# Recurrent-memory attention and a gated FFN on one core: own and early value tiles merged for 64-row products, and the normalisation of the segment outputs divided between VectorE and ScalarE

## The chip, the core and the metric

The kernel runs on one core of a Trainium2 chip. Its engines are TensorE (PE; its weight loads are a row of their own, PEld), VectorE (DVE), ScalarE (ACT), GpSimd (POOL) and the sequencer SyncE (SP), which issues most of the DMAs. The metric is the device time of one execution in microseconds; less is better. Three runs of the kernel before took 1026.67 to 1027.17 us, with a median of 1027.08.

## What is computed

A sequence of 2048 rows of 640 is normalised, cut into 64 segments of 32 rows, and run through attention with 32 heads of 128. Each segment has 8 memory rows ahead of its 32 own rows; the memory of a segment is the output of the segment before it at the memory rows, so the segments form a chain. Then a gated FFN of width 1728 follows.

```
mem = mem0
for s in range(n_seg):
    h = concat([mem, layernorm(x)[s]])           # 8 + 32 rows
    q, k, v = h @ Wq, h @ Wk, h @ Wv             # 32 heads of 128
    p = softmax(where(mask, q @ k.T * scale, -1e9))
    o = (p @ v) @ Wo
    mem, out[s] = o[:8], o[8:]
h  = x + out
h2 = h + ((relu(g) * u) @ W_down)                # g, u = layernorm(h) @ W_gate, @ W_up
```

(`gate * (gate > 0)` is written as `relu` here.)

## The kernel before

**Order of the work.** All operations are appended by `add` to one list, in program order; `_Graph.solve` works out the semaphore waits from the keys that an operation reads and writes, and each engine runs its own operations in that order. A wait on an engine therefore holds everything behind it on that engine, and so does a DMA that waits on SP. There is no planner: the order is the order of the calls.

**Own and early rows.** A segment's tile of projections has 32 columns: 8 memory rows and the first 24 of its 32 own rows. The last 8 rows of each of four segments, which do not depend on the memory, are projected ahead, for four segments together ("early", tiles `Ke`, `Qe`, `Ve`, `act_e`, two buffers each, one for a block of four). So keys and values of a segment come from two tiles: `Ko` and `Vp` (own, `a = 0`) and `Ke` and `Ve` (early, `a = 1`, of which a mask lets through the segment's own rows and those ahead of it in the block). The early projections, and for every fourth segment a pass `woe_pass` over outputs, are cut into three parts and put between the steps of the chain (`filler`).

**Layout.** Heads stand as `head(k, g)`: `g` is a group of 32 partitions (0 to 3), `k` counts 0 to 7 within it. `Vp` and `Ve` are 128 x 8 x 130: partition group `g` has the 32 rows of the values of that group's heads, column 128 is 1 (it gives the softmax's sum). `Px` holds the exponentials, 128 x 512: own ones in columns 0 to 255, early ones in 256 to 511.

**A segment (the loop over `s` from line 898 on), around the change:**

1. K is projected in two halves (`project`, matmuls on lines 374 and 357); ScalarE copies each half from PSUM to `tok[0]`, `tok[1]` (`to_tok`, line 395) and VectorE transposes it into `Ko` (`flip`, line 390).
2. `pv_x(s - 1, 0)`, line 638: the outputs of the 32 query rows of the segment before. For each of two halves `kh`, for own and early, for four columns `c` of the array and four row groups `g`, one product of 32 rows x 32 columns with 129 moving columns: 64 products, own and early summed in PSUM, into banks 0 to 3. Then `norm_x`, line 648 (reciprocal) and line 651 (two multiplications into `ox`, 128x512 each), on VectorE.
3. Q is projected in two halves, copied to `tok[2]`, `tok[3]` by ScalarE and transposed into `Qo` by VectorE; then `flip_ox(s - 1, (0,))`, line 535, transposes the first half of `ox` into `oT`.
4. V half 0 is projected and copied to `Vp[s % 2]`; `scores(s, 0)` (line 460); V half 1; `scores(s, 1)`. `scores` writes own products to columns 0 to 159 and early ones to columns 160 to 319 of a bank, each head group to its partition group.
5. `exp_mem`, `mask_mem` (lines 476, 482), `flip_ox(s - 1, (1,))`, `pv_mem` (line 513, the outputs of the memory rows), `norm_mem`, `flip_mem`, `exp_x`, `mask_x` (line 494), the fillers.
6. The output projection `wo_split`, `wo_pass` (lines 572, 555) and `to_act_split` (lines 595, 596), which writes the next segment's memory rows; `rows_split` and `store_attn` send the rows to DRAM (`attn_d`, four DMAs on SP).

Segment 0 is written out ahead of the loop, with its `pv_x` and `norm_x` there, while the weights are still arriving; the loop calls `pv_x(s - 1, 0)` from `s = 2` on. The last `pv_x` is called behind the loop, on banks 4 to 7. In segments 35, 39, 43 and 47 a transposing load, a store to `xn2_d`, and loads of `xt` and `at` for the FFN's first rows go through SP; in the segment after each, POOL adds `xt` and `at` and SP stores the sum to `h_d`.

```python
for kh in range(2):
    for a in range(2):
        for c in range(4):
            k = 4 * kh + c
            for g in range(4):
                pe.matmul(bank(b0 + g)[32*c:32*c+32, 129*kh:129*kh+129],
                          Px[32*g:32*g+32, 256*a + 32*k:256*a + 32*k + 32],
                          (t0, t1)[a][32*g:32*g+32, k, 0:129], start=(a == 0), stop=(a == 1), ...)
```

Of the kernel before, what the change touches and what calls it, by code (L numbers as in the profile page):

```python
# [163 lines left out]
def build_kernel(nc, A_x, A_mem0, A_Wq, A_Wk, A_Wv, A_Wo, A_seg_len, B_W_gate, B_W_up, B_W_down, out):  # L164
# [57 lines left out]
    mca = ar.alloc("mca", [128, 5, SEG], BF16)  # L222
    act_r = [ar.alloc(f"act_r{i}", [128, 4, DC, 32], BF16) for i in range(2)]
    act_e = [ar.alloc(f"act_e{i}", [128, DC, 32], BF16) for i in range(2)]
    tok = [ar.alloc(f"tok{i}", [128, 512], BF16) for i in range(4)]
# [5 lines left out]
    Vp = [ar.alloc(f"Vp{i}", [128, 8, VW], BF16) for i in range(2)]  # L231
# [8 lines left out]
    ox = ar.alloc("ox", [128, 4, 2, Dh], BF16)  # L240
    wtok = [ar.alloc(f"wtok{i}", [128, DC, 32], BF16) for i in range(2)]
# [36 lines left out]
    for i in (1, 0):  # L278
        add("pool", lambda p, i=i: p.memset(wtok[i][:], 0.0), w=[("wtok", i)])
# [4 lines left out]
    for i in range(2):  # L284
        add("dve", lambda v, i=i: v.memset(oT[i][:], 0.0), w=[("oT", i, n, kh) for n in "mx" for kh in range(2)])
        add("pool", lambda p, i=i: p.memset(act_r[i][:], 0.0),
            w=[("act", i, j, "m") for j in range(4)] + [("act", i, "x")] + [("act", i, "x", j) for j in range(4)])
        add("pool", lambda p, i=i: p.memset(ap(Vp[i], Dh, [[VW, 8], [1, VW - Dh]]), 1.0), w=[("Vp1", i)])
        add("pool", lambda p, i=i: p.memset(ap(Ve[i], Dh, [[VW, 8], [1, VW - Dh]]), 1.0), w=[("Ve1", i)])
        add("pool", lambda p, i=i: p.memset(act_e[i][:], 0.0), w=[("acte", i)])  # L290

    add("pool", lambda p: p.memset(mca[:], BIG), w=[("mca",)])
    for g in range(4):
        for n in range(5):
            sl = mca[32 * g:32 * g + 32, n, :]
            add("pool", lambda p, sl=sl, n=n: p.affine_select(sl, sl, [[1, SEG]], ALU.is_ge, 0.0,
                                                              base=M if n == 0 else M * (n - 1) - RID,
                                                              channel_multiplier=-1), r=[("mca",)], w=[("mca",)])
            if n > 1:
                add("pool", lambda p, sl=sl, n=n: p.affine_select(sl, sl, [[0, SEG]], ALU.is_ge, 0.0,  # L300
                                                                  base=-M * (n - 1), channel_multiplier=1),
                    r=[("mca",)], w=[("mca",)])
    add("pool", lambda p: p.memset(mbd[:], 0.0), w=[("mbd",)])
    for g in range(4):
        add("pool", lambda p, g=g: p.memset(mbd[32 * g:32 * g + 32, :, 8 * g:8 * g + 8], BIG), r=[("mbd",)], w=[("mbd",)])
        for n in range(1, 5):
            sl = mbd[32 * g:32 * g + 32, n, :]
            add("pool", lambda p, sl=sl, n=n: p.affine_select(sl, sl, [[0, 32]], ALU.is_ge, 0.0, base=-M * (n - 1),
                                                              channel_multiplier=1), r=[("mbd",)], w=[("mbd",)])
            add("pool", lambda p, sl=sl, n=n: p.affine_select(sl, sl, [[0, 32]], ALU.is_ge, 0.0, base=M * n - 1,  # L310
                                                              channel_multiplier=-1), r=[("mbd",)], w=[("mbd",)])
# [51 lines left out]
    def project(act, akeys, j, halves, banks, chunks=range(5)):  # L363

        def f(pe):
            for c in chunks:
                for n, i in enumerate(halves):
                    for g in range(4):
                        o = 2048 * i
                        w = (W[:, j, c, o + 512 * g:o + 512 * g + 512] if j == 2 else  # L370
                             W[:, j, c, o:o + 2048].rearrange("p (h e) -> p h e", e=128)[:, :, 32 * g:32 * g + 32])
                        a = (bank(banks[n])[32 * g:32 * g + 32, :], act[:, c, :], w)
                        if n == 0 or not HOLD:
                            ins = pe.matmul(*a, start=(c == 0), stop=(c == DC - 1), skip_group_check=True)  # L374
                        else:
                            ins = again(pe, *a, c == 0, c == DC - 1, g)
            return ins
        add("pe", f, r=list(akeys) + [("W", j, c) for c in chunks], w=[B(b) for b in banks] + [("Wdone", j)])

    def to_tok(b, t, eng):  # L380
        copy_op(eng, tok[t][:, :], bank(b), [B(b)], [("tok", t)])
# [7 lines left out]
    def flip(t, dst, i, keys):  # L389
        add("dve", lambda v: v.transpose(dst[:, 16 * i:16 * i + 16, 0:32], tok[t][:, :].rearrange("p (h f) -> p h f", f=32)),  # L390
            r=[("tok", t)], w=keys)
# [58 lines left out]
    def scores(s, hf):  # L450
# [3 lines left out]
        def f(pe):  # L454
            for k in range(4 * hf, 4 * hf + 4):
                for a in range(2):
                    for g in range(4):
                        h = head(k, g)
                        o = 160 * a + 40 * (k % 4)
                        i = pe.matmul(bank((P0, P1)[hf])[32 * g:32 * g + 32, o:o + 40],  # L460
# [13 lines left out]
    def exp_mem(s, hf):  # L474
        _, j = place(s)
        add("act", lambda a: a.activation(ap(Pm, 32 * hf, [[64, 2], [8, 4], [1, 8]]), s_view(hf, 0, M), ACTF.Exp,
                                          scale=SCALE), r=[B((P0, P1)[hf])], w=[("Pm", hf)])

    def mask_mem(s, hf):
        _, j = place(s)  # L480
        for i in (1, 0):
            add("dve", lambda v, i=i: v.tensor_tensor(ap(Pbd, 256 * i + 128 * hf, [[32, 4], [8, 4], [1, 8]]),
                                                      ap(Pm, 64 * i + 32 * hf, [[8, 4], [0, 4], [1, 8]]),
                                                      ap(mbd, 32 * (1 + j) * i, [[0, 4], [8, 4], [1, 8]]), ALU.min),
# [7 lines left out]
    def mask_x(s):  # L492
# [3 lines left out]
                                             ap(mca, 0, [[32 * (1 + j), 2], [0, 8], [1, 32]]), ALU.min),  # L496
            r=[("Px", 0), ("Px", 1), ("mca",)], w=[("Px", 0), ("Px", 1)])

    def v_of(s, a):
        par, p = s % 2, place(s)[0]  # L500
        if a == 0:
            return Vp[par], [("Vp", par, i) for i in range(2)] + [("Vp1", par)]
        return Ve[p], [("Ve", p, i) for i in range(2)] + [("Ve1", p)]

    def pv_mem(s, hf):
# [10 lines left out]
        (vp, e), par = place(s), s % 2  # L516
        add("pe", f, r=[("Pbd", a, hf) for a in range(2)] + [("Ve", vp, hf), ("Ve1", vp), ("Vp", par, hf), ("Vp1", par)],
# [14 lines left out]
    def flip_ox(s, halves=(0, 1)):  # L532
        p = (s + 1) % 2
        for kh in halves:
            add("dve", lambda v, kh=kh: v.transpose(ap(oT[p], 160 * kh + M, [[320, 4], [40, 4], [1, 32]]),  # L535
                                                       ap(ox, 128 * kh, [[256, 4], [1, 4], [4, 32]])),
                r=[("ox", kh)], w=[("oT", p, "x", kh)])
# [90 lines left out]

    def pv_x(s, b0):
        (t0, k0), (t1, k1) = v_of(s, 0), v_of(s, 1)  # L630

        def f(pe):
            for kh in range(2):
                for a in range(2):
                    for c in range(4):
                        k = 4 * kh + c
                        for g in range(4):
                            i = pe.matmul(bank(b0 + g)[32 * c:32 * c + 32, 129 * kh:129 * kh + 129],  # L638
                                          Px[32 * g:32 * g + 32, 256 * a + 32 * k:256 * a + 32 * k + 32],
                                          (t0, t1)[a][32 * g:32 * g + 32, k, 0:129], start=(a == 0), stop=(a == 1),  # L640
                                          skip_group_check=True, tile_position=(32 * g, 32 * c))
            return i
        add("pe", f, r=[("Px", 0), ("Px", 1)] + k0 + k1, w=[B(b0 + g) for g in range(4)])

    def norm_x(b0):
        src = ps[:, b0 * 512:b0 * 512 + 2048].rearrange("p (g r) -> p g r", r=512)[:, :, 0:258].rearrange(
            "p g (k d) -> p g k d", d=129)
        add("dve", lambda v: v.reciprocal(rx[:, :].rearrange("p (g k) -> p g k", k=2), src[:, :, :, 128]),
            r=[B(b0 + g) for g in range(4)], w=[("rx",)])
        for kh in range(2):  # L650
            add("dve", lambda v, kh=kh: v.tensor_tensor(ox[:, :, kh, :], src[:, :, kh, 0:128],  # L651
                                                      ap(rx, kh, [[2, 4], [0, 128]]), ALU.mult),
                r=[B(b0 + g) for g in range(4)] + [("rx",)], w=[("ox", kh)])
# [35 lines left out]
    for g in range(4):  # L689
        dma(wtok[1][32 * g:32 * g + M, :, :],  # L690
            mem0_ap.rearrange("t (c g j) -> g t c j", g=4, j=32)[g], r=[("wtok", 1)], w=[("wtok0", g)], eng="act")
# [18 lines left out]
    copy_op("dve", w0, wtok[1][:].rearrange("p c t -> p (c t)"), [("wtok", 1)] + [("wtok0", g) for g in range(4)],  # L710
# [156 lines left out]
    for n in range(2):  # L867
        for i in range(2):
            to_v(OB[2][n][i], Vp[0] if n else Ve[1], i, ("Vp", 0) if n else ("Ve", 1), ("act", "dve")[i])
# [3 lines left out]
    pv_x(0, P0)  # L873
# [4 lines left out]
    norm_x(P0)  # L878
    flip_ox(0)
# [18 lines left out]
    for s in range(1, NSEG):  # L898
# [16 lines left out]
        if s > 0:  # L915
            a, ks = pass_act(s)
            for i in range(2):
                project(a, ks, 1, (i,), ((P2, P3)[i],))
                to_tok((P2, P3)[i], i, "act")
                if last and i == 1:  # L920
                    load_piece(("tok", i), "act")
# [10 lines left out]
            if s > 1:  # L932
                pv_x(s - 1, 0)
                norm_x(0)
# [5 lines left out]
            if s > 1:  # L940
# [5 lines left out]
            to_v(P2, Vp[par], 0, ("Vp", par), "act")  # L946
            if last:
                load_piece(("Vp", par, 0), "act")
# [10 lines left out]
        if last:  # L959
            to_v(P3, Vp[par], 1, ("Vp", par), "act")  # L960
# [12 lines left out]
        if s > 0:  # L973
            if s > 1:
                flip_ox(s - 1, (1,))
            to_v(P3, Vp[par], 1, ("Vp", par), "act")
# [41 lines left out]
        if s >= 1:  # L1018
            rows_split(P3, P1, wtok[par], ("wtok", par))
            store_attn(wtok[par], ("wtok", par), M, 32 * (s - 1), RID)  # L1020
# [111 lines left out]
    norm_x(P0)  # L1132
    flip_ox(s)
# [109 lines left out]
```

## Time and profile before

| | |
|---|---|
| median of 3 runs | 1027.08 us (1026.67 to 1027.17) |
| the profiled execution | 1026.84 us, its span 1025.1 us |
| granted TensorE clock, mean | 0.998 |
| VectorE, ScalarE, GpSimd busy | 716.0, 501.5, 168.8 us |
| `pv_x`, line 638 | 4096 products, 4% of the chain that ended last |
| projections, line 374 | 47% of that chain |

The profile shows one execution. A group line gives the source line, engine, operation, tiles written and read, shapes and count; the timeline gives the same in order of time with start and length; the chain view follows back, from the last instruction, what each step waited for. A matmul line's form "128*32 128x512" means 128 rows and 32 columns of the array, 128 partitions and 512 columns of moving data. Starts of matmuls are recorded; their ends are modelled, and consecutive matmuls overlap.

### The profile page before, as it was taken

The page shows a single profiled execution, that of the slowest core. Times are in us where ns is not written, and L with a number is a line of the kernel's source. Part 1 is how long each engine was busy: PE and PEld are TensorE (multiplying, and loading weights), DVE is VectorE, ACT ScalarE, POOL GpSimd, SP SyncE. Part 2 cuts the span into 40 slices and gives each one's busy share as a digit, 9 for nine tenths or more (in the row PEclk, how much of TensorE's full clock was granted, in tenths as well). Part 3 has the DMA queues.
Part 4 walks back from the last instruction along what each step waited for, and adds up shares of the span by engine and source line. Part 5 has one row for each costly group of instructions (what it writes and reads, how often), then busy time and mean ns, then how long its engine had stood idle before and what let it go on. Part 6 is the DMA issues. An engine that isn't in the chain of part 4 may idle for free.

```text
span 1025.1 us, 57915 instructions
## 1 busy us (share of the span) xinstructions
PE 994.6 (97%) x27201; PEld 559.5 (55%) x26104; DVE 716.0 (70%) x1796; ACT 501.5 (49%) x1262; POOL 168.8 (16%) x402
## 2 busy tenths in 40 slices
PE   4789999999999999999999999999999999999998
PEld 1255656565656565656565566656565554444443
DVE  2558787878778787888888778787777765355332
ACT  1345555555555555565556555555555542121220
POOL 6020202120202020222222222121210010000000
PEclk9999999999999999999999999999999999999999
DMA  9920100010001001111212111000000048413100
GB/s 372 416 68 6 21 7 21 7 22 7 21 7 22 7 21 12 29 18 23 46 27 32 28 32 22 20 8 16 9 6 8 8 114 242 130 27 90 27 14 26
DMA packets 58531, 52.23 MB, mean 51 GB/s; under 512 B 37840, under 2 KB 55216, under 8 KB 56368
## 3 DMA queue, kind: packets, MB, share of 16 engines
q1 hardware_dynamic: 56160, 47.23, 16.7%
q8 instruction: 208, 3.41, 1.4%
q10 hardware_dynamic: 2128, 1.31, 0.5%
q14 instruction: 35, 0.29, 0.1%
HBM read 37.04 MB, written 6.55 MB: 43 GB/s over the span
## 4 chain that ended last, share of the span: by engine, by line
PE 93%; SPq 3%; DMA 2%; issue 0%; DVE 0%; ACT 0%; DVEq 0%; ACTq 0%
PE ps L374 47%; PE ps L817 11%; PE ps L555 7%; PE ps L572 7%; PE ps L357 6%; PE ps L638 4%; PE ps L615 4%; SPq L320 3%; PE ps L1049 3%; PE ps L460 3%; DMA Wo<-in_A_Wo_dram 2%; PE ps L513 2%; PE ps L830 0%; PE ps L1061 0%; DVE TBf L595 0%
## 5 line engine op out<-in xcount | busy, mean ns | idle before, releaser
L374 PE MATMUL ps<-W,act_r 128*32 128x512 bf16 x7580 | 448.3, 381 | 2.1 <-DVE act_r L596 1.4
L374 PEld LDWEIGHTS ps<-W,act_r 128*32 128x32 bf16 x7580 | 190.6, 96 | 201.5 <-DVE act_r L596 31.2
L395 ACT ACTIVATE tok<-ps 128x512 bf16<-128x512 f32 x324 | 189.0, 597 | 163.5 <-PE ps L374 134.4
L374 PE MATMUL ps<-W,act_e 128*32 128x512 bf16 x1224 | 121.2, 383 | 7.5 <-DMA W<-in_A_Wv_dram 4.0
L468 POOL COPY Qo<-Qe 128x256 bf16<-128x256 bf16 x64 | 31.8, 497 | 547.4 <-DVE oT L529 524.4
L390 DVE STREAM_TRANSPOSE Ko<-tok 128x512 bf16<-128x512 bf16 x128 | 89.6, 701 | 40.0 <-ACT tok L395 36.9
L395 ACT ACTIVATE Vp<-ps 128x512 bf16<-128x512 f32 x127 | 75.8, 597 | 69.2 <-PE ps L374 69.2
L390 DVE STREAM_TRANSPOSE Qo<-tok 128x512 bf16<-128x512 bf16 x126 | 88.9, 706 | 14.1 <-ACT tok L395 14.1
L535 DVE STREAM_TRANSPOSE oT<-ox 128x512 bf16<-128x512 bf16 x128 | 87.8, 687 | 0.0
L357 PE MATMUL ps<-W,act_e 128*32 128x512 bf16 x856 | 87.7, 385 | 0.0
L555 PE MATMUL ps<-Wo,oT 128*32 128x160 bf16 x4032 | 83.3, 233 | 1.0 <-issue 0.6
L651 DVE TENSOR_TENSOR ox<-ps,rx 128x512 bf16<-128x512 f32 x128 | 82.5, 687 | 2.2
L572 PE MATMUL ps<-Wo,oT 128*32 128x320 bf16 x2016 | 81.2, 299 | 0.0
L555 PEld LDWEIGHTS ps<-Wo,oT 128*32 128x32 bf16 x4032 | 75.7, 97 | 5.8 <-DMA Wo<-in_A_Wo_dram 1.3
L585 ACT ACTIVATE SA<-TA 64x40 f32<-64x40 f32 x126 | 29.5, 234 | 84.9 <-DVE TA L583 84.2
L845 ACT ACTIVATE g<-ps 128x512 bf16<-128x512 f32 x52 | 30.1, 593 | 82.8 <-PE ps L817 82.8
L817 PE MATMUL ps<-xn2T,Wu 128*128 128x512 bf16 x260 | 64.6, 379 | 0.0
L846 DVE TENSOR_TENSOR hT<-g,ps 128x512 bf16<-128x512 bf16 x52 | 35.8, 688 | 40.5 <-PE ps L817 40.1
L572 PEld LDWEIGHTS ps<-Wo,oT 128*32 128x32 bf16 x2016 | 56.4, 96 | 13.8 <-issue 1.1
L374 PEld LDWEIGHTS ps<-W,act_e 128*32 128x32 bf16 x1224 | 37.1, 97 | 47.8 <-issue 34.8
L817 PE MATMUL ps<-xn2T,Wg 128*128 128x512 bf16 x246 | 61.6, 379 | 1.5 <-issue 1.1
L529 DVE STREAM_TRANSPOSE oT<-om 128x128 bf16<-128x128 bf16 x126 | 39.2, 311 | 29.4 <-ACT om L524 28.1
(109 smaller groups left out, 1359.1 us busy)
## 6 DMA issues: line engine op xcount, KB each, us to landing
W<-in_A_Wk_dram SPq DMA_DIRECT2D x5, 1024.0 KB
W<-in_A_Wq_dram SPq DMA_DIRECT2D x5, 1024.0 KB
W<-in_A_Wv_dram SPq DMA_DIRECT2D x5, 1024.0 KB
Wo<-in_A_Wo_dram SPq DMA_DIRECT2D x8, 640.0 KB
attn_d<-wtok SPq DMA_DIRECT2D x248, 7.5 KB
xt<-in_A_x_dram SPq DMA_DIRECT2D x16, 160.0 KB
at<-attn_d SPq DMA_DIRECT2D x16, 160.0 KB
out_dram<-osb SPq DMA_DIRECT2D x15, 160.0 KB
```

Of the source, the lines that this page charges most:

```text
L357: return pe.add_instruction(mybir.InstMatmult(name=nc.get_next_instruction_name(), engine=mybir.EngineType.PE, ins=[pe.lower_ap(rhs), pe.l ...
L374: ins = pe.matmul(*a, start=(c == 0), stop=(c == DC - 1), skip_group_check=True)
L390: add("dve", lambda v: v.transpose(dst[:, 16 * i:16 * i + 16, 0:32], tok[t][:, :].rearrange("p (h f) -> p h f", f=32)), r=[("tok", t)], w= ...
L395: add("act", lambda a: a.activation(dst, src, ACTF.Copy), r=r, w=w)
L529: add("dve", lambda v: v.transpose(ap(oT[par], 160 * hf, [[40, 4], [320, 4], [1, 8]]), ap(om, 128 * hf, [[1, 4], [4, 32]])), r=[("om", hf) ...
L535: add("dve", lambda v, kh=kh: v.transpose(ap(oT[p], 160 * kh + M, [[320, 4], [40, 4], [1, 32]]), ap(ox, 128 * kh, [[256, 4], [1, 4], [4, 3 ...
L555: i = pe.matmul(bank(bk)[32 * gg:32 * gg + 32, 0:160], src[:, hb, 0:32], w[:, gg], start=(hb == CH[16 * halves[0]]), stop=(hb == CH[-1]), ...
L572: i = pe.matmul(bank(bk)[32 * q:32 * q + 32, 0:320], src[:, hb, 0:32], w, start=(n == 0), stop=(n == 7), skip_group_check=True)
L615: ins = pe.matmul(bank(bk)[32 * q:32 * q + 32, 0:320], src[:, hb, 0:32], w[:, 2 * (q % 2):2 * (q % 2) + 2], start=(i == 0), stop=(i == 15) ...
L638: i = pe.matmul(bank(b0 + g)[32 * c:32 * c + 32, 129 * kh:129 * kh + 129], Px[32 * g:32 * g + 32, 256 * a + 32 * k:256 * a + 32 * k + 32], ...
L651: add("dve", lambda v, kh=kh: v.tensor_tensor(ox[:, :, kh, :], src[:, :, kh, 0:128], ap(rx, kh, [[2, 4], [0, 128]]), ALU.mult), r=[B(b0 + ...
L817: ins = pe.matmul(bank(bk), w[:, c, lo:lo + 128], xn2T[par][:, c, :], start=(c == 0), stop=(c == DC - 1))
```

## The change

- `merge_v`: DMAs on SP copy own and early values into two merged tiles `VM[0]`, `VM[1]` of 128 x 8 x 130. `VM[r]` has, in partition group `g`, the own values where `g % 2 == r` and the early values elsewhere. To make neighbouring groups belong to the same heads, the early V projection swaps neighbouring groups (`swap`), and `scores` writes early products of group `g` to partition group `g ^ 1` and sorts its columns by `g % 2`. One `merge_v` is four DMAs of 32 partitions. The own ones are called in each segment once both halves of `Vp` are written, the early ones in every fourth segment behind `pv_x`.
- `pv_x` then takes 64 rows at a time, 32 products, with no sum in PSUM. The masks `mca`, `mbd` are laid out anew (more instructions on POOL at the start), and `exp_mem` and `mask_mem` address by the new order, with the same element counts.
- `norm_x` keeps the reciprocal and the first multiplication. The second is cut: `norm_x_late` multiplies half of it on VectorE and the other half in two ScalarE copies with a scale. It is called, with `flip_ox(s - 1, (0,))`, between the two halves of the Q projection; before, `flip_ox` came behind both.
- Segment 0's `pv_x` and `norm_x` move into the loop (`s = 1`).
- Space: `ox` shares a tile `tox` with `tok[0]` and `tok[1]`; `Vp` and `wtok` have one buffer instead of two.

```diff
     def project(act, akeys, j, halves, banks, chunks=range(5)):
+        swap = 1 if j == 2 and akeys[0][0] == "acte" else 0
...
-                        w = (W[:, j, c, o + 512 * g:o + 512 * g + 512] if j == 2 else
+                        w = (W[:, j, c, o + 512 * (g ^ swap):o + 512 * (g ^ swap) + 512] if j == 2 else
...
                 for a in range(2):
                     for g in range(4):
                         h = head(k, g)
-                        o = 160 * a + 40 * (k % 4)
-                        i = pe.matmul(bank((P0, P1)[hf])[32 * g:32 * g + 32, o:o + 40],
+                        o, q = 160 * (g % 2) + 40 * (k % 4), 32 * (g ^ a)
+                        i = pe.matmul(bank((P0, P1)[hf])[q:q + 32, o:o + 40],
...
+    def merge_v(s, a):
+        (t, ks), flat = v_of(s, a), "p k d -> p (k d)"
+        for r in range(2):
+            for g in range(4):
+                if g % 2 == r ^ a:
+                    dma(VM[r][32 * g:32 * g + 32].rearrange(flat), t[32 * g:32 * g + 32].rearrange(flat), r=ks,
+                        w=[("VM", r, g)])
...
             for kh in range(2):
-                for a in range(2):
+                for r in range(2):
                     for c in range(4):
                         k = 4 * kh + c
-                        for g in range(4):
-                            i = pe.matmul(bank(b0 + g)[32 * c:32 * c + 32, 129 * kh:129 * kh + 129],
-                                          Px[32 * g:32 * g + 32, 256 * a + 32 * k:256 * a + 32 * k + 32],
-                                          (t0, t1)[a][32 * g:32 * g + 32, k, 0:129], start=(a == 0), stop=(a == 1),
-                                          skip_group_check=True, tile_position=(32 * g, 32 * c))
+                        for u in range(2):
+                            i = pe.matmul(bank(b0 + 2 * u + r)[32 * c:32 * c + 32, 129 * kh:129 * kh + 129],
+                                          Px[64 * u:64 * u + 64, 256 * r + 32 * k:256 * r + 32 * k + 32],
+                                          VM[r][64 * u:64 * u + 64, k, 0:129], start=True, stop=True,
+                                          skip_group_check=True, tile_position=(64 * u, 32 * c))
...
+    def norm_x_late(b0):
+        src = ps[:, b0 * 512 + 1024:b0 * 512 + 2048].rearrange("p (g r) -> p g r", r=512)[:, :, 129:257]
+        add("dve", lambda v: v.tensor_tensor(tox[:, 2:4, 1, :], src, ap(rx, 5, [[2, 2], [0, 128]]), ALU.mult),
+            r=[B(b0 + 2), B(b0 + 3), ("rx",)], w=[("ox", 1, 1)])
+        for g in range(2):
+            add("act", lambda a, g=g: a.activation(tox[:, g, 1, :], bank(b0 + g)[:, 129:257], ACTF.Copy,
+                                                   scale=rx[:, 2 * g + 1:2 * g + 2]),
+                r=[B(b0 + g), ("rx",)], w=[("ox", 1, 0)])
...
-            if s > 1:
-                pv_x(s - 1, 0)
-                norm_x(0)
+            pv_x(s - 1, 0)
+            norm_x(0)
+            if s % 4 == 2:
+                merge_v(s, 1)
             if not last:
                 for i in range(2):
                     project(a, ks, 0, (i,), ((P0, P1)[i],))
                     to_tok((P0, P1)[i], 2 + i, "act")
                     flip(2 + i, Qo, i, [("Qo", i)])
-            if s > 1:
+                    if i == 0:
+                        norm_x_late(0)
+                        flip_ox(s - 1, (0,))
...
         if s > 0:
-            if s > 1:
-                flip_ox(s - 1, (1,))
-            to_v(P3, Vp[par], 1, ("Vp", par), "act")
+            flip_ox(s - 1, (1,))
+            to_v(P3, Vp, 1, ("Vp",), "act")
+            merge_v(s, 0)
```

## The prediction

> **What bounds the kernel now.** I read the page first: the engines' shares and the chain that ended last.
>
> ```profile
> span 1025.1 us, 57915 instructions
> PE 994.6 (97%) x27201; PEld 559.5 (55%) x26104; DVE 716.0 (70%) x1796; ACT 501.5 (49%) x1262; POOL 168.8 (16%) x402
> PE 93%; SPq 3%; DMA 2%; issue 0%; DVE 0%; ACT 0%; DVEq 0%; ACTq 0%
> ```
>
> TensorE (PE) carries 93% of the chain. What is not PE (SPq and DMA) lies ahead of 57 us, while the weights arrive. Next I asked for the chain in the middle of the recurrence, 300 to 360 us: every piece is PE, one behind another, and a segment takes 12.40 us.
>
> ```profile
> 305.86 2.21 PE ps L374 x40
> 308.07 0.66 PE ps L638 x64
> 308.73 3.35 PE ps L374 x60
> 312.08 0.25 PE ps L460 x31
> ```
>
> So in segments 2 to 63 a nanosecond off PE is a nanosecond off the span, until another engine is late. L638 is `pv_x`, 64 products of 32 rows each. Then the timeline of PE around that piece (columns: start, length, line, shapes, count), and the same in slices of 0.02 us; the two lines from slices are the ones with x6 and the x4 that starts at 307.68.
>
> ```profile
> 307.68 0.39 PE L374 MATMUL ps<-W,act_r 128*32 128x512 bf16 x4
> 308.00 0.24 PE L638 MATMUL ps<-Vp,Px 32*32 32x129 bf16 x6
> ...
> 308.00 0.28 PE L638 MATMUL ps<-Vp,Px 32*32 32x129 bf16 x16
> 308.07 0.28 PE L638 MATMUL ps<-Ve,Px 32*32 32x129 bf16 x16
> 308.25 0.35 PE L638 MATMUL ps<-Vp,Px 32*32 32x129 bf16 x16
> 308.38 0.35 PE L638 MATMUL ps<-Ve,Px 32*32 32x129 bf16 x16
> 308.66 3.42 PE L374 MATMUL ps<-W,act_r 128*32 128x512 bf16 x60
> ```
>
> The call has three parts. From the last start of L374 (307.69) to the first of L638 (308.00) 0.309 us pass: 512 columns (0.213, since four such products share a pitch of 0.215) and a pause of 0.096 that appears at no change between two 128*32 forms. Then 64 starts in 0.510. Then 0.153 to the next L374: 129 columns (0.054) and again 0.099. In all 0.972, the same to 1 or 2 ns in 61 of the 62 calls at L638 that stand between L374 (segment 54's took 1.113). Inside the 0.510, six products start within 0.02 us, one per 3.3 ns; the second round of sixteen starts 0.067 behind the first (129 columns and 0.013 more). After about 33 pairs of weight load and matmul nothing starts until 308.25, and from there one pair starts per 8.3 ns: whatever was queued is used up, and PE runs at the rate of its issue.
>
> **The PE term.** After the change the call has 32 products of 64 rows and 32 columns of the array: 8 places of the array, 4 rounds. The form 64*32 is not in the trace. The nearest rows are L638 itself and the only 64-row products, L1061.
>
> ```profile
> 924.19 0.30 PE L357 MATMUL ps<-Wd,hT 128*128 128x320 bf16 x1
> 924.43 0.45 PE L1061 MATMUL ps<-Wd,hT 64*128 64x320 bf16 x4
> 924.80 0.31 PE L1049 MATMUL ps<-Wd,hT 128*128 128x320 bf16 x1
> ```
>
> Here two products in the two row halves start together (924.43, x2 in a narrower window) and the next two 0.147 later: the halves do run beside each other, and a round is its 320 columns (0.133) plus 0.014. The changes of form cost 0.232 and 0.229, that is the columns and 0.096 to 0.099 as above. So I take for the new call 0.309 before, 3 rounds of 0.067 plus 7 starts of 0.0033 = 0.224 from first to last start, and 0.153 behind: 0.686 instead of 0.972, **0.286 less**. All 32 pairs fit into the 33 that were queued, so the slow issue does not show. Bounds: a round of 0.0565 if weight loads hide (L513, 129 columns, has about that pitch) gives 0.193 and a gain of 0.317; issue at 8.3 ns throughout gives 0.258 and 0.252. I take 0.067, the row of the same columns and tile width. Times 63 calls on the chain (segments 2 to 63 and the last one): 18.0 us, from 15.9 to 20.0.
>
> **What is moved.** The call for segment 0 stood at 45.21, under the Wo load (chain: DMA to 55.5 us), free. It moves into segment 1, which has no such call: 0.686 less the 0.205 that L374 takes anyway, **+0.48**, once (0 to 0.7).
>
> **scores.** Same 64 products a segment, but early ones swap the array's column groups, so a group comes again after 3 or 5 places instead of 4. At 838.00 a queued call shows 25 ns a round of four; one more start (3.3 ns) a round makes 8 rounds 0.226, and a call takes 0.241 from first to last start now, as its last pair is issued late. I take 0; a whole pair (8.3 ns) in each of 16 rounds would be 0.13 a segment. Fewer than none is excluded: nothing is taken out.
>
> **VectorE and ScalarE.** With `pv_x` at 308.00, today's rows:
>
> ```profile
> 308.75 0.71 DVE L390 STREAM_TRANSPOSE Ko<-tok 128x512 bf16<-128x512 bf16 x1 [0.37 <-ACT tok L395]
> 309.39 0.17 DVE L648 RECIPROCAL rx<-ps 128x8 f32<-128x8 f32 x1
> 309.59 1.29 DVE L651 TENSOR_TENSOR ox<-ps,rx 128x512 bf16<-128x512 f32 x2
> 310.79 0.70 DVE L390 STREAM_TRANSPOSE Qo<-tok 128x512 bf16<-128x512 bf16 x1
> 311.68 0.71 DVE L390 STREAM_TRANSPOSE Qo<-tok 128x512 bf16<-128x512 bf16 x1 [0.19 <-ACT tok L395]
> ```
>
> The reciprocal waits for the second K flip, not for PE, so it stays at 309.39. One product ends at 310.27. ScalarE has the first Q half out at 310.29 (0.29 sooner), so its flip runs 310.32 to 311.02. Then the late half-product (128x256; L602's 128x160 takes 0.325 and L1070's 128x320 0.485, so about 0.4) to 311.4, the x flip (0.67) to 312.0, and the second Q flip, now behind it, to 312.65 instead of 312.39. The second `scores` needs that flip and comes at 313.25 - 0.29 = 312.96: 0.3 to spare, where 0.86 was. ScalarE takes two 128x128 copies (L524: 0.368) between its evictions, so the second Q eviction starts at 310.95 instead of 310.77; that is inside the above. The first memory mask then ends at 312.95 and its reader, L513, comes at 313.21. So all is covered; past 0.3 us each 0.1 us costs 6.3 us over 63 segments. The wait put on ScalarE's x copies (for rx) has the second Q eviction queued behind it, but rx is there at 309.56.
>
> **Merging.** Four copies of 32 partitions x 2080 bytes a segment on SP, four more every fourth segment. Today four such issues take 1.53 us (`attn_d`, 306.36), 0.38 each. The own values are complete when ScalarE ends at 314.07; issued by 315.6; SP's rows show a landing awaited for up to 3.4 us (behind the transposing load), so 317.6 to 319.0. `pv_x` asks at 320.25. Cover 1.2 us. The early ones follow `pv_x` and have the segment. Every copy is one more semaphore for PE (the trace's semaphore instructions on PE take 0.051), taken by its sequencer while the K products, 2.2 us, are still queued. In segments 35, 39, 43, 47 the transposing load and what follows wait behind the copies and arrive about 7 us later; the next segment's copies then queue behind the `h_d` store until about 501.8 and land by 505.3, asked for at about 506.4. In the prologue the copies stand behind Wo in one queue, where packets go in order (the 1280-byte packets of xl go at 52 to 55, behind Wo's). The longer mask set-up on POOL (some 14 instructions of 0.2) ends near 26 us; its first reader is at 40.1.
>
> **Sum.** 63 x -0.286 + 0.48 = -17.5. The profiled execution took 1026.84 (span 1025.1 and 1.74 around it), so 1009.3; the median of the runs is 0.24 higher: **1009.5 us**.
>
> **Rivals.**
> - Loads hide (0.317): 1007.5, 10%. Issue-bound (0.252): 1011.7, 10%. Both are the bounds above.
> - The gain is partly given back on VectorE (second Q flip, 0.1 late) or in `scores` (0.1): 63 x 0.1 = 6.3, 1016. For it: the cover shrinks from 0.86 to 0.3. Against: every term has a row. 14%.
> - The merged tile saves nothing, as the two row halves take turns: 8 rounds of 0.067, first to last 0.47 against 0.51; with +0.48, 1025. Against: 924.43. 3%.
> - Slower: the copies land late, so PE waits at each `pv_x`. They cost from 4.6 us after the last issue (320.25 - 315.6) and turn the change into a loss from 4.9. At 5.7 us: 63 x (1.1 - 0.286) + 0.48 = +51.8, 1078.9. For it: no row shows a copy inside SBUF. Against: loads and stores of this size are awaited 2 to 3.4 us. 6%.
> - Slower by serial weight loads: each row group takes load and product by turns, 16 products x 0.067 in a row group, 1.005 from first to last start: 63 x 0.495 + 0.48 = +31.7, 1058.8. The present call would take as long by it, 16 products in each of four row groups, and takes 0.510. 1%. [...]
>
> **Chances.** Forecast 56%, rivals as above. About 2 us, 0.2%, is what a measurement here tells from no change. Faster 0.90, same 0.03, slower 0.07. Range 1004 to 1018: both bounds and the 6.3 us given back, with a margin; it leaves out about 10%.
>
> **What would show it.** Per call at the new `pv_x`: 0.309, 0.22, 0.153, and no gap after 33 pairs; a segment of 12.11 us; `scores` still 0.241 from first to last start; PE never idle ahead of `scores` or `pv_x`. Wrong it is if the chain shows DMA or DVE between PE pieces from 70 us on, or if the 32 starts take 0.25 and more.

## The result, and the profile after

The changed kernel takes **1012.57 us** (median of 4 runs, 1011.41 to 1014.37) against 1027.10; the ratio is 0.986, 95% interval 0.9845 to 0.9874. That is 14.5 us less; forecast were 17.5 (1009.5 us, range 1004 to 1018). The profiled execution took 1012.54 us, its span 1010.6. Lines of the code after the change: `project` L380 and L362 (were L374, L357), `pv_x` L654 (L638), `scores` L469 (L460), `flip` L399, `mask_mem` L491, `pv_mem` L522, `norm_x` L666 and L667, `norm_x_late` L672 and L675.

The page of the kernel after, its span, engines and chain by engine:

```profile
span 1010.6 us, 54471 instructions
PE 974.6 (96%) x25153; PEld 542.0 (54%) x24056; DVE 702.3 (69%) x1796; ACT 536.6 (53%) x1390; POOL 171.3 (17%) x416
PE 92%; SPq 3%; DMA 3%; DVE 1%; issue 1%; ACT 0%; DVEq 0%; ACTq 0%
```

PE has 2048 products fewer (32 in each of 64 calls) and still carries the chain. The same stretch of the chain as was shown of before:

```profile
300.34 2.21 PE ps L380 x40
302.55 0.35 PE ps L654 x32
302.90 3.35 PE ps L380 x60
306.25 0.25 PE ps L469 x32
```

PE follows on PE; `pv_x` takes 0.35 where it took 0.66, its neighbours what they took. The timeline of PE around that call, in slices (the x6 line is from a slice of 0.02 us):

```profile
302.48 0.24 PE L654 MATMUL ps<-VM,Px 64*32 64x129 bf16 x6
...
302.48 0.42 PE L654 MATMUL ps<-VM,Px 64*32 64x129 bf16 x32
```

By the trace's starts the parts are 0.309 before, **0.204** from first to last start (rounds begin at 302.481, .548, .605 and .662) and 0.147 behind: 0.660 instead of 0.972, 0.312 less, the same within 2 ns in every undisturbed call. A plain segment takes 12.09 to 12.10 us instead of 12.40. VectorE's timeline beside it:

```profile
303.87 0.17 DVE L666 RECIPROCAL rx<-ps 128x8 f32<-128x8 f32 x1
...
305.72 0.69 DVE L544 STREAM_TRANSPOSE oT<-tox 128x512 bf16<-128x512 bf16 x1
306.33 0.67 DVE L399 STREAM_TRANSPOSE Qo<-tok 128x512 bf16<-128x512 bf16 x1
```

The second Q flip ends at 307.00, and its reader, the second `scores`, starts at 307.42: covered.

Not every segment is like that. Before four `pv_x` calls PE stands still: 1.36 us at 498.64 (the call for segment 36, made in segment 37), 1.00 at 597.41 (44), 0.63 at 707.32 (53), 0.82 at 829.01 (the last). The chain around the first of them, then SP's and POOL's timelines ahead of it:

```profile
495.07 2.24 PE ps L380 x40
...
497.33 0.60 ACT tox L404
...
498.64 0.42 PE ps L654 x32
```

```profile
492.98 0.34 SPq L325 DMA_DIRECT2D h_d<-xt  x1
493.42 2.45 SPq L325 DMA_DIRECT2D VM<-Vp  x4
```

```profile
491.55 1.40 POOL L686 TENSOR_TENSOR xt<-xt,at 128x640 bf16<-128x640 bf16 x1 [9.07 <-DMA at<-attn_d]
```

The chain names ScalarE, but what it did there (the second K eviction, and two short pieces for the FFN's first rows) is nothing that `pv_x` reads, and in a plain segment `pv_x` starts (302.48) ahead of that eviction (302.60). The four copies' last packet ends at 497.93, and PE goes 0.71 later; so the cause is read to be the DMA, and an experiment below bears it out for segments 36 and 44. For segment 53 it is a reading: PE goes 0.71 behind the copies' last packet there too, but also 1.23 behind a packet of instructions, as in the pauses of the last section. `Vp` was complete at 490.86. SP could issue only at 493.42, because it stood before the `h_d` store, which waits for POOL's addition, which waits for the load of `at`. In before the same addition waited for nothing but its own place (VectorE's second K flip), the load being there:

```profile
496.15 1.40 POOL L662 TENSOR_TENSOR xt<-xt,at 128x640 bf16<-128x640 bf16 x1 [4.17 <-DVE Ko L390]
```

(By the traces the additions run in segments 32, 36, 40 and 44, the loads of `xt` and `at` in 31, 35, 39 and 43, and the transposing loads in 35, 39, 43 and 47; lists of the additions that run from 36 to 48 are one block late.) In segment 35 the load of `at` is issued 7.7 us behind the start of that segment's `pv_x` call in before (482.20, 489.90), and 16.1 behind it now (473.01, 489.15). So the copies of one segment push the FFN's loads back on SP, these the addition, this the store, and the store the next segment's copies.

### The profile page after: what moved, and what is told of

Its sections match the earlier page's. It is cut to its first block, busy times and chain, and to the rows that moved or that the text cites. A ratio compares the mean times of both kernels' runs of the same rounds, so it can differ in the third digit from the quotient of the medians.

```text
span 1010.6 us, 54471 instructions
## 1 busy us (share of the span) xinstructions
PE 974.6 (96%) x25153; PEld 542.0 (54%) x24056; DVE 702.3 (69%) x1796; ACT 536.6 (53%) x1390; POOL 171.3 (17%) x416
## 4 chain that ended last, share of the span: by engine, by line
PE 92%; SPq 3%; DMA 3%; DVE 1%; issue 1%; ACT 0%; DVEq 0%; ACTq 0%
PE ps L380 47%; PE ps L841 10%; PE ps L564 7%; PE ps L581 7%; PE ps L362 6%; PE ps L624 4%; SPq L325 3%; PE ps L1078 3%; PE ps L469 3%; PE ps L654 2%; DMA Wo<-in_A_Wo_dram 2%; PE ps L522 2%; DMA Wd<-in_B_W_down_dram 0%; PE ps L854 0%; PE ps L1090 0%
## 5 line engine op out<-in xcount | busy, mean ns | idle before, releaser
L380 PE MATMUL ps<-W,act_r 128*32 128x512 bf16 x7580 | 448.3, 380 | 2.4 <-ACT tok L404 1.2
L380 PEld LDWEIGHTS ps<-W,act_r 128*32 128x32 bf16 x7580 | 192.9, 96 | 202.5 <-DVE act_r L605 31.4
L404 ACT ACTIVATE tok<-ps 128x512 bf16<-128x512 f32 x190 | 109.3, 594 | 62.5 <-PE ps L380 53.6
L380 PE MATMUL ps<-W,act_e 128*32 128x512 bf16 x1224 | 121.3, 384 | 7.4 <-DMA W<-in_A_Wv_dram 4.0
L399 DVE STREAM_TRANSPOSE Ko<-tox 128x512 bf16<-128x512 bf16 x128 | 89.7, 702 | 39.6 <-ACT tox L404 38.7
L404 ACT ACTIVATE tox<-ps 128x512 bf16<-128x512 f32 x134 | 79.6, 598 | 54.4 <-PE ps L380 33.4
L544 DVE STREAM_TRANSPOSE oT<-tox 128x512 bf16<-128x512 bf16 x128 | 89.3, 699 | 0.0
L399 DVE STREAM_TRANSPOSE Qo<-tok 128x512 bf16<-128x512 bf16 x124 | 85.6, 690 | 4.8 <-ACT tok L404 2.4
L362 PE MATMUL ps<-W,act_e 128*32 128x512 bf16 x856 | 87.4, 386 | 0.0
L841 PE MATMUL ps<-xn2T,Wu 128*128 128x512 bf16 x259 | 64.5, 379 | 0.1
L841 PE MATMUL ps<-xn2T,Wg 128*128 128x512 bf16 x247 | 61.8, 379 | 1.3 <-issue 1.0
L380 PEld LDWEIGHTS ps<-W,act_e 128*32 128x32 bf16 x1224 | 37.0, 98 | 47.4 <-issue 33.0
```

The lines of the kernel that those rows point to most:

```text
L362: return pe.add_instruction(mybir.InstMatmult(name=nc.get_next_instruction_name(), engine=mybir.EngineType.PE, ins=[pe.lower_ap(rhs), pe.l ...
L404: add("act", lambda a: a.activation(dst, src, ACTF.Copy), r=r, w=w)
L841: ins = pe.matmul(bank(bk), w[:, c, lo:lo + 128], xn2T[par][:, c, :], start=(c == 0), stop=(c == DC - 1))
```

## The experiments

Each is an edit of the changed kernel unless it says otherwise, timed beside the kernel before on the same chip.

**Where the gain is from.** The old call was read as limited by PE's issue; the array's rounds are the rival. In `pv_x`:

```diff
-            for kh in range(2):
+            for kh in (0, 1, 0, 1):
```

> The changed kernel with the 32 products of pv_x issued twice in a row (same output), 64 pairs of 64 rows. It asks what the old call's slow second half was. If the array's rounds set the pace (0.067 for the first change of round, 0.057 after it): 7 changes, 0.067 + 6 x 0.057 + 0.023 = 0.43 us from first to last start, a call of 0.89, +0.23 a segment, 1012.5 + 14.5 = 1027. If PE's issue sets it (as read from before: some 33 pairs queued, a pause, then 8.3 ns a pair): 0.25 + 31 x 0.0083 = 0.51 us from first to last start, a call of 0.97, +0.31 a segment, 1012.5 + 19.8 = 1032. Longer segments also give the late copies more time, up to 4 us off both.

1035.77 us (1034.97 to 1036.29), ratio 1.0089 (1.0073 to 1.0104). The call has 0.512 us from first to last start and 0.976 in all: issue, to 2 ns. Two slices of its timeline:

```profile
297.80 0.42 PE L654 MATMUL ps<-VM,Px 64*32 64x129 bf16 x32
...
297.82 0.71 PE L654 MATMUL ps<-VM,Px 64*32 64x129 bf16 x57
```

The first 32 products start within 0.205; the 33rd starts 0.049 later, at 298.055, and from there one starts per 8.3 ns. In before the break stands at the same place, by the starts: the 33rd product comes 0.252 behind the first, here 0.254. 64 pairs of 64 rows take 0.512, 64 pairs of 32 rows took 0.510: here the rows do not matter, the number of pairs does. A call is 0.316 longer, so 64 calls give 20.2; the rest of the 22 us between the profiled spans is irregular: of segments 2 to 62, taken from one `pv_x` to the next, those that are more than 0.12 us over the median length are so by 9.2 us in all, against 6.8 in the changed kernel. That the first 32 pairs stand queued is the author's reading; the traces show the break behind the 32nd start, in both kernels.

**The normalisation**, once alone in the kernel before (`norm_x_late` and the x flip between the Q flips, 64 products as they were), once taken out of the changed kernel (one 128x512 multiplication on VectorE, x flip behind both Q flips):

```diff
             norm_x(0)
+            norm_x_late(0)
...
-                    if i == 0:
-                        norm_x_late(0)
-                        flip_ox(s - 1, (0,))
+            flip_ox(s - 1, (0,))
```

> The kernel before with only the second part of the change: a quarter of the x normalisation on ScalarE between its evictions, the late half-product on VectorE, and the x flip between the two Q flips; no merged tiles, pv_x with its 64 products. Theory (PE sets the period, VectorE and ScalarE are covered on either side): 1027 us within 1, a segment of 12.40 us as before. Rival (the divided normalisation is worth something by itself, or costs something because ScalarE's copies delay the second Q eviction): at least 0.1 us a segment, so 1021 or less, or 1033 or more.

> The second multiplication of the normalisation stands whole on VectorE right behind the first, and the first x flip comes behind both query flips, as before the change; merged tiles and 64-row products stay. Theory (VectorE has slack between the key flips and the memory mask, so this half of the change is worth nearly nothing): 0 to 0.05 us a segment, 1012.6 to 1016; a segment without stalls still takes 12.09 to 12.15 us. Rival (with the shorter product VectorE would set the pace, and the split is what lets the gain through): 0.1 us a segment or more, 1019 to 1031, and PE waits for DVE between scores and the output projection in every segment.

Alone: 1026.11 us (1024.64 to 1027.28, 10 runs), ratio 0.9993 (0.9984 to 1.0003), a segment 12.40 to 12.41. Taken out: 1012.10 (1011.43 to 1012.34), ratio 0.9858 (0.9845 to 0.9872), a segment 12.09. This part is worth nothing measurable either way; both sides were covered.

**What the copies cost.** `merge_v` returns at once for `s > 0`:

> The copies into the merged tiles are made for segment 0 alone; every later pv_x multiplies with segment 0's values, so the outputs of the x rows are not the reference's, at the same number of products. Theory (copies cost only where they are late: 1.4, 1.1, 0.7 and 0.9 us before four pv_x): 4.1 us less, 1008.5. Rival (copies also slow the steady segments, by the SBUF, the DMA engines or instruction fetches): steady segments fall below 12.09 us and the time below 1007.5.

1007.69 us (1007.37 to 1008.19), ratio 0.9816 (0.9803 to 0.983); no wait ahead of `pv_x` is left, and all four additions on POOL wait for VectorE's second K flip again, as in before. So the copies take back some 4.9 us of the gain (4.7, if each kernel is taken against its own before). For the waits in segments 36 and 44 the store was moved behind the copies:

```diff
-                dma(h_d[128 * e2:128 * e2 + 128, :], xt[:, :], r=[("xt",)], w=[("h_d", e2)])
             pv_x(s - 1, 0)
...
             merge_v(s, 0)
+            if s % 4 == 0 and e2 is not None:
+                dma(h_d[128 * e2:128 * e2 + 128, :], xt[:, :], r=[("xt",)], w=[("h_d", e2)])
```

> The h_d store of segments 32, 36, 40 and 44 is issued behind the segment's four copies into the merged tiles instead of ahead of them; nothing else differs from the changed kernel. Theory (the copies are late there because SP stands at the h_d store, which waits for POOL's sum): in segments 36 and 44 the copies are issued within 0.1 us of the end of ScalarE's last copy into Vp instead of 2.6 and 2.7 us later, the waits of 1.36 and 1.00 us before the following pv_x go, and the time falls by 2.4 us, from 1012.6 to about 1010.2. Rival (the DMA engines themselves are late, by the loads of xt and at and by instruction packets): the waits stay and so does the time, 1012.6.

1010.97 us (1010.31 to 1012.19), ratio 0.985 (0.9836 to 0.9863). SP's timeline in segment 36:

```profile
491.73 3.62 SPq L325 DMA_DIRECT2D VM<-Vp  x4
495.39 0.58 SPq L325 DMA_DIRECT2D h_d<-xt  x1
```

The waits in segments 36 and 44 are gone (`pv_x` follows L380 by the usual 0.309), though in segment 36 the issues began 0.64 us behind ScalarE's end, not 0.1, and took 3.62. The times alone do not settle it, since the intervals of the two ratios overlap; the trace does. What is left is 1.24 us ahead of the last `pv_x`. For that one, the FFN's weight piece that ScalarE's queue loads beside the copies goes to SP, behind them (the second line stands ahead of the last `pv_x`; the edit above is in this kernel too):

```diff
-            load_piece(("g1", 0), "act")
...
+    load_piece(("hT", 0, 0))
```

> The changed kernel with the h_d store behind the segment's four copies (as in the earlier run) and the FFN weight piece that ScalarE's queue loads in the last segment issued on SP instead, behind those copies. Theory (the last segment's copies are held up on the DMA engines by that piece): the wait ahead of the last pv_x, 0.8 to 1.6 us, goes; 1010.0 us within 0.7. Rival (instruction packets hold them up, or the piece is needed as early as it came): 1011 as with the store alone, or more if the FFN's first product then waits for its weights.

1010.98 us (1010.48 to 1011.30), ratio 0.9847 (0.9833 to 0.9862). The mechanism came out, the time did not. Its chain at the last call:

```profile
827.87 0.35 PE ps L654 x32
```

It follows on L841 without a wait. The rival's number is met, but the profiled execution does not show its reason: it has 2.0 us of pauses in which PE waits for nothing that the profile shows, against 0.98 in the run before it, 0.54 us of waits ahead of `pv_x` of segments 35 and 53, where that run has none (whether from late copies or from such pauses is not told apart), and 0.41 ahead of `act_r` in segment 36 (there 0.12). That is one execution of each; the median may have other reasons.

**The start.** Segment 1's first product comes 0.54 later than before (57.22, now 57.76); Wo's last packet ends at 55.55 instead of 55.08, and segment 0's copies have packets from 53.79 on. So segment 0's copies were made to wait for Wo's last load:

```diff
-        merge_v(0, a)
+        merge_v(0, a, [("Wo", 1, 3)])
```

> Segment 0's eight copies wait for the landing of the last Wo load; before, they were queued behind it without a wait. Theory (they mingle with the tail of Wo on the DMA engines and delay its landing by about 0.5 us): the last Wo product starts near 55.6 us instead of 56.54 and segment 1's first product near 57.2 instead of 57.76; 1012.1. Rival (Wo ends late for another reason, an instruction packet): segment 1 still starts near 57.8, 1012.6.

1014.81 us (1013.97 to 1015.89), ratio 0.9886 (0.9872 to 0.99). Wo's last packet ends at 55.03, as without the copies; the eleven profiles with copies queued behind Wo have 55.53 to 56.47. Segment 1 does start 0.96 earlier, and then waits for its copies, by the timeline of PE:

```profile
62.18 0.42 PE L654 MATMUL ps<-VM,Px 64*32 64x129 bf16 x32 [3.03 <-DMA VM<-Vp]
```

The late start is the smaller price: 0.54 here, up to 1.2 in the other profiles with queued copies, where segment 1 starts at 57.8 to 58.4.

**The copies without the wait.** The waits ahead of `pv_x` account for 3.8 of the 4.9 us. Is there a cost in the traffic itself? All copies are issued, into a tile that `pv_x` does not read:

```diff
+                    d = r if s == 0 else 1
-                    dma(VM[r][32 * g:32 * g + 32].rearrange(flat), t[32 * g:32 * g + 32].rearrange(flat), r=ks,
+                    dma(VM[d][32 * g:32 * g + 32].rearrange(flat), t[32 * g:32 * g + 32].rearrange(flat), r=ks,
...
-                                          VM[r][64 * u:64 * u + 64, k, 0:129], start=True, stop=True,
+                                          VM[0][64 * u:64 * u + 64, k, 0:129], start=True, stop=True,
```

> The changed kernel with all its copies issued and moved as now, but from segment 1 on into a tile that nobody reads, and pv_x reads segment 0's merged values throughout (so later outputs are not the reference's). The copies keep their traffic and their place on SP; what goes is PE's wait for them. Theory (the copies cost time only where pv_x waits for one): as without any copies, 1007.7 us within 0.7. Rival (their traffic on the DMA engines disturbs by itself, by the h_d store, the Wo load or the instructions that PE fetches, so that its irregular pauses grow): 1009.0 or more.

1009.98 us (1007.87 to 1011.23), ratio 0.984 (0.9826 to 0.9853): the rival, and the trace shows what. VectorE and POOL in segment 40 (`mask_mem` twice, then the addition):

```profile
539.32 0.36 DVE L491 TENSOR_TENSOR Pbd<-Pm,mbd 128x128 bf16<-128x128 bf16 x2
...
540.65 1.56 DVE L491 TENSOR_TENSOR Pbd<-Pm,mbd 128x128 bf16<-128x128 bf16 x2 [0.19 <-ACT Pm L485]
```

```profile
540.74 1.40 POOL L687 TENSOR_TENSOR xt<-xt,at 128x640 bf16<-128x640 bf16 x1 [8.61 <-DMA at<-attn_d]
```

Two multiplications that take 0.36 elsewhere take 1.56 here, where POOL's addition begins among them, and end at 542.21, the addition at 542.14; `pv_mem` comes 0.95 late. With 0.57 and 0.76 in segments 36 and 44 that is 2.28 us. Without copies the addition ran at 535.38 to 536.78, under PSUM multiplications and flips, which kept their length (0.69 and 0.71). The late addition is the same one that held the store. In the changed kernel it meets `mask_mem` once (segment 40, PE 0.30 late). So the addition was moved, first behind `mask_x`, with the store behind it:

```diff
-                add_attn(xt[:, :], xt, at, [("xt",), ("at",), ("Ko", 1)], [("xt",)], "pool")
...
         mask_x(s)
+        if s % 4 == 0 and e2 is not None:
+            add_attn(xt[:, :], xt, at, [("xt",), ("at",), ("Px", 1)], [("xt",)], "pool")
```

> The kernel with unread copies, and the additions of x and attention rows on POOL in segments 36, 40, 44 and 48 (with their h_d stores) made to wait for the segment's mask_x instead of its second K flip. As before it, the copies go into a tile that nobody reads and later outputs are not the reference's. Theory (what was left of the copies' cost is one collision: they push the loads of xt and at back, so that the 1.40 us addition on POOL falls on mask_mem, which takes 1.2 to 1.4 us in place of 0.22, and PE waits 0.57 to 0.95 ahead of pv_mem): these three waits go, 2.3 us less, 1007.7. Rival (the copies' traffic disturbs whatever POOL does): stays at 1010.

1012.31 us (1011.35 to 1014.30), ratio 0.9857 (0.984 to 0.9873): the expectation missed, 2.3 us over the kernel that it changes (the intervals overlap). No wait ahead of `pv_mem` is left, but POOL's own step towards the next segment's `act_r` now stands behind the addition:

```profile
495.68 1.40 POOL L687 TENSOR_TENSOR xt<-xt,at 128x640 bf16<-128x640 bf16 x1 [0.17 <-POOL oTe L553]
497.24 0.27 POOL L596 TENSOR_TENSOR SA<-SA,TA 128x40 f32<-128x40 f32 x1 [0.17 <-POOL xt L687]
```

Four segments are 1.20 us longer. The same in the kernel with the other two mends:

> The changed kernel with all three mends: the additions on POOL and the h_d stores behind mask_x, so behind the segment's four copies too, and the last weight piece on SP behind the last copies. Theory: the waits ahead of pv_x in segments 36, 44 and 63 are gone (3.2 us) and the collision of the addition with mask_mem (0.24 us, segment 40) and with mask_x; 1010.7 us within 0.7, irregular pauses left. If the addition now meets something on VectorE that PE waits for, 1011.5 or more.

1013.61 us (1011.24 to 1015.06), ratio 0.9863 (0.984 to 0.9885), with the same four waits. Then the addition waited for the last `mask_mem` (`("Pbd", 0, 1)` in place of `("Px", 1)`, the three lines moved behind `mask_mem(s, 1)`):

> The kernel with unread copies again, with the additions on POOL (and their h_d stores) waiting for the segment's last mask_mem, so that they run between it and POOL's copies for the next segment (Qo, oTe, SA). Later outputs are not the reference's, as before. Theory (the addition costs PE time only where it lies on mask_mem, or ahead of POOL's own part of the chain to act_r): neither the waits ahead of pv_mem (2.3 us in the three segments of the first kernel with unread copies) nor those ahead of act_r (4 x 1.2 us in the second) remain; 1007.7 us within 0.8. Rival (something else of the copies' traffic): 1009.5 or more.

1009.70 us (1007.53 to 1011.24), ratio 0.9824 (0.9808 to 0.9841). VectorE and POOL in segment 40 again:

```profile
540.97 0.36 DVE L491 TENSOR_TENSOR Pbd<-Pm,mbd 128x128 bf16<-128x128 bf16 x2 [0.19 <-ACT Pm L485]
```

```profile
541.41 1.41 POOL L687 TENSOR_TENSOR xt<-xt,at 128x640 bf16<-128x640 bf16 x1 [8.98 <-DVE Pbd L491]
```

The collision with `mask_mem` is gone in all four segments, and the wait ahead of `act_r` in three; in segment 44 `at` landed so late that the addition lay on `mask_x` (1.40 instead of 0.38, PE 0.70 late). The time fell by only 0.3 us, and by its number the rival is met: 1.7 us remain to the kernel without copies (17.6 and 19.2 under their own before), with overlapping intervals. In the two profiled executions (1009.82 and 1008.01) PE's pauses without an awaited event come to 2.1 and 0.5 us, which is most of the difference; whether the copies bring them about is not shown. Last, all mends with the copies read:

> The kernel with the three mends, the additions placed in the same way (behind mask_mem instead of behind mask_x). Theory: the 4 x 1.2 us ahead of act_r go, and the 0.24 of segment 40 too; 1010.0 to 1011.0 us, what is left against a kernel without copies being irregular pauses of PE and an occasional late copy.

**1009.71 us** (1008.82 to 1012.52), ratio 0.9834 (0.9817 to 0.985): the lowest median of the kernels that compute everything, 2.9 us under the change as it was; the intervals of the two ratios just overlap, and against the store alone (0.985) no gain is shown. The median is a little under the expected range. The profiled execution still has 0.69 us of waits ahead of `pv_x` of segments 15 and 45, 0.40 ahead of `act_r` in segment 36, where the addition lay on `mask_x` (1.10 instead of 0.38), and one pause of 1.36.

## Why the prediction was right, and where it was short

- **The PE term** was right in kind and 0.026 us a call too small. Its parts measured 0.309, 0.204 and 0.147 where it had 0.309, 0.224 and 0.153. The mis-sized step is "3 rounds of 0.067": only the first change of round takes 0.067, the other two 0.057 as in the lower bound that was given (0.193). 63 x 0.026 = 1.6 us more gain. "All 32 pairs fit into the 33 that were queued" holds with nothing to spare: by the starts the break in before lies behind the 32nd pair, not behind a 33rd.
- **Segment 0's call in segment 1**: +0.48 forecast, +0.47 measured (11.646 to 12.116, between the first K products of segments 1 and 2).
- **scores**: 0.242 from first to last start, forecast 0.241.
- **VectorE and ScalarE**: the reciprocal starts 1.39 behind the first start of `pv_x`, as forecast; the second Q flip ends 4.52 behind it (forecast 4.65) and its reader starts 4.94 behind (4.96). Covered with 0.42 to spare.
- **Merging** failed in two places. Four issues were put at 1.53 us; they take 2.4, and up to 3.7 where a 16384-byte instruction packet lies among them (3.66 in segment 53, one of the waits). The last packet ends 1.10 after the last issue, or 1.5 to 3.3 when such a packet or another queue's load lies among them. In a plain segment 0.9 to 3.0 us lie between the last packet and `pv_x`, which needs 0.5 to 0.7 of them. Not in segments 36 and 44: the step "land by 505.3, asked for at about 506.4" found the queue behind the `h_d` store, but gave the copies 3.5 us from issue to use where 5.2 and 4.9 passed, and had them issued 4.6 us ahead of PE's asking where it was 3.8. Those two waits, the one of segment 53 and the last sum to 3.81 us. The last call's neighbours were left out of the forecast: ScalarE's weight piece loads there.
- **Nothing was said of POOL's addition coming late.** The seven microseconds of delay on SP were found and followed to the store, not to what the addition would meet on VectorE: 0.30 us here, 2.3 in the kernel with unread copies.
- **Start**: "packets go in order" behind Wo was wrong; +0.54. The row given for it is misread: in before the 1280-byte packets of `xl` run from 53.39 to 55.50, and Wo's last ends at 55.08, so they mingle there as well.
- **The sum** of the measured terms: -17.5 - 1.6 + 0.54 + 3.81 + 0.30 = -14.5, and the span fell by 14.5. That they agree so closely is partly luck: the sum leaves out PE's own pauses (0.93 us here, 0.57 before), other irregular segments of both executions, and segment 27, which is 0.35 longer in all twelve kernels with merged tiles, the one without copies included. There VectorE's last step to `act_r` (line 605) starts 0.43 late without waiting for anything that the profile shows; why stays open. And the forecast erred by +1.6 and by -4.65, which partly cancel.
- **Rivals**: "loads hide" is the closest for the PE term (0.317; measured 0.312). Late copies, named as the slower rival, did occur, in 4 calls of 63 (one of them, segment 53's, by the reading above). Turns of the row halves and serial weight loads are excluded by the 0.204. So is the rate of issue, whose 1011.7 lies nearest to the measured time: its 0.258 from first to last start was not seen.
- **Signs**: of what was to show the forecast, the segment (12.10) and the call came out; one sign of being wrong appeared too, as the chain has waits between PE's pieces behind 70 us, in segments 27 and 40 and ahead of the four calls.

## What to carry to other kernels

Where many short products follow one another, count pairs before columns: here the first 32 pairs of a call, which are read as queued, start at 3.3 ns a pair within a round, and those beyond at 8.3. A DMA put into a queue is also paid by what stands behind it there (here the load of `at` was issued 16.1 us behind the start of segment 35's `pv_x` instead of 7.7): follow each of those to the engine that uses it and to what that engine then runs beside. Before moving such an operation, list both what it may collide with and what its own engine has to do next.

## What the runs showed of the hardware that was not expected

- Beside POOL's addition of `xt` and `at`, both in SBUF, VectorE's multiplications with two SBUF inputs took longer: with unread copies `mask_mem` 1.16, 1.42 and 1.36 us instead of 0.22, ending within 0.1 of POOL's end, and in the changed kernel `mask_x` 0.56 and 0.72 instead of 0.38 (segments 36 and 44), while flips (0.70, the small ones 0.31), reciprocals (0.17) and multiplications from PSUM (0.69) beside it kept their length. What holds them up is not shown.
- The changed kernel's instruction queue moved 193 packets of 16384 bytes:

```profile
q8 instruction: 193, 3.16, 1.3%
```

 PE and PEld records, the sequencer's included, are 49467 there and 53398 in before with 208 packets: 256.3 and 256.7 a packet, so they are read as PE's instructions. In all fourteen profiles the 35 pauses of 0.15 us and more, from 60 us to the FFN's products, in which PE waited for no event (nor for a copy) end 1.28 to 1.58 us after the end of such a packet (1.44 and 1.46 in before, 1.42 in the changed kernel). One of them in the chain of the changed kernel, where the packet ends at 813.53:

```profile
813.90 0.13 PE ps L624
814.02 0.93 issue
814.95 1.00 PE ps L624 x23
```

 A packet comes every 5 us, so that place would be met by chance about 6 times in 100. That PE waits for its instructions is the reading; no run changed the fetch, so it is not shown. Whether the copies make these pauses longer stays open: 0.35 to 0.57 us in the three kernels without copies, 0.25 to 2.5 in those with.
- Copies inside SBUF (65 KB each) take SP 0.59 us to issue, the `attn_d` stores to DRAM (7.5 KB) 0.37 and the `h_d` store (160 KB) 0.34, so it is not the size alone.
